# One half of an output projection with the activations standing and the weight streaming in four column tiles, in a decode kernel on one Trainium2 core

## Chip, core and metric

The kernel runs on one core of one Trainium2 chip. The metric is the device time of one execution in microseconds (us); several executions of the kernel are timed and their median is the time. The profile used beside it is one further execution, recorded by the hardware profiler.

## What is computed

One decode step for 8 sequences (B = 8, one token each, D = 512). Only the last W = 2048 positions of the two caches are read. Cut to what matters:

```python
x = A_x                                               # 8 x 1 x 512
h = x + attention(layernorm(x), k_cache, v_cache, wq) @ wo
# attention: 32 query heads of 128, 8 key/value heads, softmax over 2048 positions
# wo: 4096 x 512, so the projection sums over 32 heads x 128
u = layernorm(h)
h2 = h + u + gelu(layernorm(u) @ w3) @ w4             # w3: 512 x 1792, w4: 1792 x 512
```

The token-shift branch with w1 and w2 is identically zero for one token and isn't computed.

## The kernel before, in words

**Units.** The attention is cut into 16 units n = 0..15: unit n is sequence b = n // 2 and half t = n % 2 of the eight key/value heads (16 query heads). Each unit loads 2 MB of keys (`knat`) and 2 MB of values (`vnat`). All loads of caches and weights are issued by SyncE (SP) from one function, line 204, into one DMA queue, so that they land nearly in the order of issue: the last of them are the values of unit 15, the second half of wo, two pieces of w3 and four pieces of w4.

**Main loop (lines 549 to 593).** Keys are turned on TensorE by fp32 transposes (line 313), copied out by ScalarE and VectorE (lines 300 and 301) and multiplied with the queries in four column tiles of 32 (line 328: 32 columns standing, 512 moving). Softmax runs once for a sequence. The values are multiplied three units late (line 425; for the last three units line 415 with the values standing). `fold` and `turn_o` bring a unit's result into `o2`: on VectorE the scaling (line 448) and a spread (line 455), on TensorE a turn in four column tiles (line 464), on VectorE a mask (line 471) and a sum (line 477). `o2[:, t, j, b]` then holds, on 128 partitions, element block j (of 16) of half t of sequence b.

**Output projection.** `pe_wo(t)` (lines 508 to 516) multiplies half t of wo (2048 rows, seen as 16 blocks j of 128 rows). For every j and each of four column blocks nb it loads a 128 x 128 block of wo as the standing operand and streams the 8 columns of `o2[:, t, j, :]` past it: 64 pairs of a weight load and a matmul for a half, all accumulated in `hT_ps`, which is 128 partitions x 32 (four blocks nb x 8 sequences), so that the result h lies transposed. Before it, `pe_wo_x` (line 504) adds x into the same place.

**Order at the end (lines 608 to 615).** Each engine works its list in the order in which the program appends to it. For TensorE the end of the list is: line 415 for the last unit, `pe_wo(0)`, the turn of the last unit (line 464), `pe_wo(1)`, then layernorm sums (lines 640 and 662), w3 (line 657), one fp32 matmul that puts the residual into `z_ps` (line 682) and w4 in four column tiles (line 691). `pe_wo(0)` waits for the sum of unit 14 (line 477) and for the first half of wo, loaded since unit 7; `pe_wo(1)` waits for the sum of unit 15 and for the second half of wo (`sem_wl`). On ScalarE the last entry before the tail is a one-element square root (line 615), which loads the table that lines 663 and 664 need. Lines 700 and 702 copy the result out, line 705 stores it.

Two more things that the change uses: `oE`, a 128 x 512 fp32 tile which in the main loop takes the copied-out value products (line 434) for `fold` (line 443: fp32 matmuls with 128 columns of `oE` standing and 16 columns of `selo` moving); and `selo`, 128 x 32, with a one where the partition number modulo 32 equals the column.

Of the kernel before, what the change touches and what calls it, by code (L numbers as in the profile page):

```python
# [6 lines left out]
dt = mybir.dt  # L7
ACT = mybir.ActivationFunctionType
ALU = mybir.AluOpType
AX = mybir.AxisListType  # L10

B = 8
# [11 lines left out]
KC = D // 128  # L24
# [4 lines left out]
NU = 2  # L29
# [11 lines left out]
KR = 16  # L41
# [6 lines left out]
NST = 3  # L48
# [33 lines left out]
def bass_sequential_preLN__sliding_block_cached__mixer_s_mlp__decode_kernel(  # L82
# [19 lines left out]
    NUN = NB * NU  # L102
# [4 lines left out]
    with es:  # L107
        sb = lambda shape, dtype, name: es.enter_context(nc.sbuf_tensor(name, shape, dtype))
# [7 lines left out]
        wo_v = wbig[:, :].rearrange("p (t j n) -> p t j n", t=NU, j=KR)  # L116
# [44 lines left out]
        oM = sb([128, KR, QR], dt.bfloat16, "oM")  # L161
        oE = sb([128, 512], dt.float32, "oE")
        selo = sb([128, MO], dt.float32, "selo")
        o2 = sb([128, NU, KR, B], dt.bfloat16, "o2")

        NH = KC * B
        tail = Pz[:, 0, :].bitcast(dt.float32)
# [2 lines left out]
        def tl(n, bf=False):  # L170
# [14 lines left out]
        kbank = [kT_ps[i // 2][:, (i % 2) * 1024:(i % 2 + 1) * 1024].bitcast(dt.float32) for i in range(4)]  # L185
# [10 lines left out]
        sem_wl = S("sem_wl")  # L196
        sem_w3 = [S(f"sem_w3{i}") for i in range(2)]
        sem_x, sem_wq, sem_wo, sem_w4a, sem_w4b, sem_w4c, sem_out = (
            S(n) for n in ("sem_x", "sem_wq", "sem_wo", "sem_w4a", "sem_w4b", "sem_w4c", "sem_out"))
        PE, AC, DV, PO, SP = (Engine(S(n)) for n in ("s_pe", "s_act", "s_dve", "s_pool", "s_sp"))  # L200

        def dma(eng, dst, src, sem, *waits):
            def f(e):
# [7 lines left out]
        e_iota = PO.op(lambda e: e.iota(iota_f, [[1, 128]], base=0, channel_multiplier=-1,  # L211
                                        allow_small_or_imprecise_dtypes=True))
        e_qz = PO.op(lambda e: e.memset(qz[:], 0.0))
        PO.op(lambda e: e.memset(ones_f[:], 1.0))
        PO.op(lambda e: e.memset(ones_m[:], -1.0 / D))
        PO.op(lambda e: e.memset(eps2[:], EPS * EPS))
# [5 lines left out]
        e = DV.op(lambda e: e.bn_stats(st6[:, :], x_sb[:, :]), X)  # L222
        e = DV.op(lambda e: e.bn_aggr(mv[:, :], st6[:, :]), e)
        e = AC.op(lambda e: e.activation(rstd[:, :], mv[:, 1:2], ACT.Sqrt, bias=eps1[0:B, :], scale=1.0), e, e_eps)
        e = DV.op(lambda e: e.reciprocal(rstd[:, :], rstd[:, :]), e)
# [6 lines left out]
        e_selo = DV.op(lambda e: e.tensor_reduce(selo[:, :], ident_f[:, :].rearrange("p (a x) -> p x a", a=TO),  # L232
                                                 AX.X, ALU.add))
# [25 lines left out]
        e = PE.op(pe_xT, e_xln, e_idb)  # L259
# [12 lines left out]
        e = DV.op(lambda e: e.tensor_scalar(q_d, S_ps[0][:, 0:H * B], inv_sqrt_dh, None, ALU.mult), e_q)  # L272
# [17 lines left out]
        e_T, e_Tlo, e_Thi, e_lo, e_hi, e_QK, e_PV = {}, [], [], [], [], {}, {}  # L290
        e_ev, e_Pz = {}, {}
        e_max, e_mT, e_neg, e_negps, e_negc, e_exp, e_PT, e_pS, e_lsel, e_Lb, e_rL, e_scale, e_sc = ({} for _ in range(13))
# [112 lines left out]
        e_ev_o, e_fold, e_turn = {}, {}, {}  # L405
# [52 lines left out]
        def turn_o(n):  # L458
            b, t = divmod(n, NU)
            dst = sm[:, 0:QR * KR]  # L460

            def f(e):
                for r in range(R):
                    ins = e.matmul(dst[32 * r:32 * (r + 1), :], mE[:, :],
                                   oK[:, n % 2, QR * r:QR * (r + 1), :].rearrange("p h j -> p (h j)"),
                                   start=True, stop=True, tile_position=(0, 32 * r), skip_group_check=True)
                return ins
            e_turn[n] = PE.op(f, e_mE, e_sc[n], sm_read[0])
            m_ap = mH[:, :]
            m_bc = bass.AP(tensor=m_ap.tensor, offset=m_ap.offset, ap=[m_ap.ap[0], [0, KR], [1, QR]])  # L470
            e = DV.op(lambda e: e.tensor_tensor(oM[:, :, :], dst.rearrange("p (h j) -> p j h", h=QR), m_bc, ALU.mult),
                      e_turn[n], e_mH, e_scale.get(n - 1))
            sm_read[0] = e

            def g(e):
                with nc.allow_low_precision(reason="one term and zeros"):
                    return e.tensor_reduce(o2[:, t, :, b], oM[:, :, :], AX.X, ALU.add)
            e_scale[n] = DV.op(g, e)

        def load_k(n):  # L480
            b, t = divmod(n, NU)
# [9 lines left out]
        def load_wo(t, sem):  # L491
            dma(SP, wo_v[:, t, :, :].rearrange("p j n -> p (j n)"),
                A_wo[128 * KR * t:128 * KR * (t + 1), :].rearrange("(p j) n -> p (j n)", j=KR), sem, e_q)

        def hcol(nb):
            at = 256 * (nb // 2) + nb % 2
            return slice(at, at + 255, 2)

        hT_ps = S_ps[0]
        e_wo = []  # L500

        def pe_wo_x(e):
            for nb in range(KC):
                ins = e.matmul(hT_ps[:, nb * B:(nb + 1) * B], x_sb[:, hcol(nb)],
                               ident_b[0:B, 0:B], start=(nb == 0), stop=False, skip_group_check=True)
            return ins

        def pe_wo(t, *waits):
            def f(e):
                for j in range(KR):  # L510
                    for nb in range(KC):
                        ins = e.matmul(hT_ps[:, nb * B:(nb + 1) * B], wo_v[:, t, j, hcol(nb)],  # L512
                                       o2[:, t, j, :], start=False, stop=(t == NU - 1 and j == KR - 1),
                                       skip_group_check=True)
                return ins
            e_wo.append(PE.op(f, *waits))

        def emit_PV(i):
            n, w = divmod(i, U)
# [19 lines left out]
        def turn_os(to):  # L539
            while turned[0] < to:  # L540
                turn_o(turned[0])
                turned[0] += 1
# [6 lines left out]
        for n in range(NUN):  # L549
# [8 lines left out]
            i = U * n  # L558
            b, t = divmod(n, NU)
# [49 lines left out]
        PE.op(pe_wo_x, e_exp[NB - 2], X)  # L609
        emit_PVs(NBLK)  # L610
        load_wo(1, sem_wl)
        pe_wo(0, e_scale[NUN - NU], (sem_wo, 16))
        turn_os(NUN)
        pe_wo(1, e_scale[NUN - 1], (sem_wl, 16))
        e_gl = AC.op(lambda e: e.activation(scratch[:, 1:2], scratch[:, 0:1], ACT.Sqrt), e_warm)

        for a in range(2):
# [16 lines left out]
        def bc(a, k=KC):  # L634
            return bass.AP(tensor=a.tensor, offset=a.offset, ap=[a.ap[0], [0, k], [1, B]])
# [6 lines left out]
        e = DV.op(lambda e: e.tensor_tensor(v3(hc[:, :]), v3(hs[:, :]), bc(st1), ALU.add))  # L642
        e = DV.op(lambda e: e.tensor_tensor(hsq[:, :], hc[:, :], hc[:, :], ALU.mult), e)
# [18 lines left out]
        e = PE.op(lambda e: e.matmul(st2, ones_v[:, :], vsum[:, :], start=True, stop=True), e_vs, e_sc[NUN - 1])  # L662
# [4 lines left out]
        e = DV.op(lambda e: e.tensor_tensor(v3(xb[:, :]), v3(hc[:, :]), bc(rr[:, B:2 * B]), ALU.mult), e_r1)  # L667
# [5 lines left out]
        for n in range(2):  # L673
            cs = slice(n * FH * B, (n + 1) * FH * B)
            gs = slice(n * FH * 32, (n + 1) * FH * 32)
            e = DV.op(lambda e, n=n, cs=cs: e.tensor_tensor(v3(g_x[:, cs]), v3(y_ps[n][:, 0:FH * B]),
                                                            bc(rr[:, 0:B], FH), ALU.mult), e_y[n], e_rr)
# [64 lines left out]
```

## Time and profile before

| What | us |
|---|---|
| median of 3 runs | 195.41 (195.14 to 195.58) |
| the profiled execution | 195.09 |
| its span, first to last instruction | 193.8 |
| outside its span | 1.29 |
| TensorE busy in the span | 145.7 (75%) |
| VectorE busy | 107.6 (56%) |
| ScalarE busy | 89.9 (46%) |
| HBM read | 79.18 MB, 409 GB/s over the span |

How to read the profile's lines. Times are from the span's start. A line of the timeline gives start, duration, engine, line of the kernel, operation, the tile written and the tiles read, shapes and a count; PE is a matmul on TensorE, PEld its weight load, DVE is VectorE, ACT is ScalarE; in brackets stands how long the engine was idle before and what ended that. "128*32" is the used part of the array (rows * columns). An fp32 matmul that isn't a transpose shows as two records for PE and two for PEld. "issue" is idle time for which the profile shows no cause. PEclk is the granted TensorE clock as a share of full speed. In the view by windows, after the length of the window, each engine has its busy time and in brackets its number of instructions; the last three columns are PEclk, DMA share and GB/s.

### The profile page before, as it was taken

What the parts mean: (1) busy time and instruction counts of PE and PEld (TensorE: products, weight loads), DVE (VectorE), ACT (ScalarE), POOL (GpSimd) and SP (SyncE); (2) the same over time, 40 slices, a digit from 0 to 9 for tenths busy, and PEclk for the clock granted to TensorE, in tenths of its full rate; (3) what the DMA queues carried; (4) which work ended last, traced back from release to release, by engine and by line L of the source; (5) the groups of instructions that cost most, each with busy time, mean ns of one, the idle gap of its engine ahead of it and who ended that gap; (6) DMA issues with size and microseconds to landing.
All of it is one profiled execution on the core that took longest, in us unless ns stands there. A gap on an engine that the chain in (4) does not pass through costs nothing.

```text
span 193.8 us, 4487 instructions
## 1 busy us (share of the span) xinstructions
PE 145.7 (75%) x1972; PEld 114.9 (59%) x1972; DVE 107.6 (56%) x281; ACT 89.9 (46%) x115; POOL 7.8 (4%) x29
## 2 busy tenths in 40 slices
PE   0028985978899799918887897886597897768675
PEld 0037862866568477608575866564585574667674
DVE  5502445476596687722966485657355965843232
ACT  6000566747547485524464636482354664250022
POOL 5001001000100100010001000100000000000000
PEclk9999999699999999975999799999879999655555
DMA  6999999999999999999999999999999999999981
GB/s 225 433 430 430 430 433 430 423 426 421 423 430 423 423 433 424 426 426 430 430 430 423 430 426 426 426 421 433 433 409 430 426 426 430 426 426 424 406 353 54
DMA packets 5954, 79.46 MB, mean 410 GB/s; under 512 B 672, under 2 KB 688, under 8 KB 1456
## 3 DMA queue, kind: packets, MB, share of 16 engines
q1 hardware_dynamic: 5920, 79.18, 96.6%
q8 instruction: 15, 0.25, 0.5%
q14 instruction: 3, 0.02, 0.0%
q10 hardware_dynamic: 16, 0.01, 0.0%
HBM read 79.18 MB, written 0.01 MB: 409 GB/s over the span
## 4 chain that ended last, share of the span: by engine, by line
DMA 51%; PE 33%; DVE 13%; issue 2%; ACT 0%; SPq 0%
DMA knat<-in_A_k_cache_dram 44%; PE kT_ps L313 17%; DMA vnat<-in_A_v_cache_dram 7%; DVE kT_sb L301 6%; PE S_ps L328 5%; DVE Pz L374 3%; PE kT_ps L385 3%; PE S_ps L512 2%; DVE mcol L338 1%; PE oT_ps L415 1%; PE kT_ps L657 1%; PE S_ps L691 1%; PE sm L443 1%; DVE Mrow L344 1%; PE sm L342 1%
## 5 line engine op out<-in xcount | busy, mean ns | idle before, releaser
L300 ACT ACTIVATE kT_sb<-kT_ps 128x1024 bf16<-128x1024 bf16 x64 | 62.8, 1023 | 42.5 <-PE kT_ps L313 42.4
L313 PE MATMUL kT_ps<-perm_k,knat 128*128 128x128 f32 x512 | 71.8, 299 | 10.0 <-DMA knat<-in_A_k_cache_dram 9.7
L313 PEld LDWEIGHTS kT_ps<-perm_k,knat 128*128 128x128 f32 x512 | 63.7, 154 | 17.4 <-DMA knat<-in_A_k_cache_dram 11.3
L301 DVE TENSOR_SCALAR kT_sb<-kT_ps 128x512 int32<-128x512 int32 x64 | 43.5, 688 | 38.4 <-PE kT_ps L313 38.3
L328 PE MATMUL S_ps<-kT_sb,qz 128*32 128x512 bf16 x256 | 19.8, 383 | 6.3 <-DVE kT_sb L301 4.2
L374 DVE TENSOR_TENSOR Pz<-P_sb,mJ 128x256 bf16<-128x256 bf16 x64 | 23.9, 417 | 0.0
L434 ACT ACTIVATE oE<-oT_ps 128x256 f32<-128x256 f32 x13 | 5.0, 384 | 27.8 <-PE oT_ps L425 27.8
L425 PE MATMUL oT_ps<-vnat,pS 128*32 128x256 bf16 x416 | 17.5, 275 | 0.3 <-DMA vnat<-in_A_v_cache_dram 0.3
L300 ACT ACTIVATE pS<-kT_ps 128x1024 bf16<-128x1024 bf16 x8 | 8.2, 1024 | 10.5 <-PE kT_ps L385 10.5
L328 PEld LDWEIGHTS S_ps<-kT_sb,qz 128*32 128x32 bf16 x256 | 4.6, 94 | 11.3 <-ACT kT_sb L300 10.2
L425 PEld LDWEIGHTS oT_ps<-vnat,pS 128*32 128x32 bf16 x416 | 9.1, 96 | 3.4 <-DMA vnat<-in_A_v_cache_dram 0.4
L301 DVE TENSOR_SCALAR pS<-kT_ps 128x512 int32<-128x512 int32 x8 | 5.5, 691 | 7.7 <-PE kT_ps L385 7.7
L385 PE MATMUL kT_ps<-perm_p,Pz 128*128 128x128 f32 x64 | 9.6, 298 | 0.0
L285 POOL COPY qz<-q_sb 64x64 bf16<-64x64 bf16 x16 | 4.7, 291 | 117.4 <-PE S_ps L328 101.6
L385 PEld LDWEIGHTS kT_ps<-perm_p,Pz 128*128 128x128 f32 x64 | 7.6, 151 | 3.0 <-issue 3.0
L267 PE MATMUL S_ps<-xlnT,wbig 128*128 128x8 bf16 x128 | 3.6, 168 | 7.7 <-DMA wbig<-in_A_wq_dram 7.7
L443 PEld LDWEIGHTS sm<-selo,oE 128*128 128x128 f32 x52 | 7.9, 217 | 0.4 <-ACT oE L434 0.4
L267 PEld LDWEIGHTS S_ps<-xlnT,wbig 128*128 128x128 bf16 x128 | 3.5, 104 | 7.7 <-issue 7.7
L415 PE MATMUL oT_ps<-pS,vnat 128*128 128x16 bf16 x192 | 6.3, 175 | 2.4 <-DMA vnat<-in_A_v_cache_dram 1.5
L338 DVE TENSOR_REDUCE mcol<-S_ps 128x1 f32<-128x512 f32 x8 | 5.5, 692 | 4.5 <-PE S_ps L328 4.5
L443 PE MATMUL sm<-selo,oE 128*128 128x16 f32 x52 | 7.7, 263 | 0.3 <-DVE negcol L356 0.3
L415 PEld LDWEIGHTS oT_ps<-pS,vnat 128*128 128x128 bf16 x192 | 5.9, 105 | 3.1 <-DMA vnat<-in_A_v_cache_dram 1.9
(93 smaller groups left out, 94.5 us busy)
## 6 DMA issues: line engine op xcount, KB each, us to landing
knat<-in_A_k_cache_dram SPq DMA_DIRECT2D x16, 2048.0 KB, 30.0
vnat<-in_A_v_cache_dram SPq DMA_DIRECT2D x16, 2048.0 KB, 34.2
wbig<-in_A_wq_dram SPq DMA_DIRECT2D x1, 4096.0 KB, 12.2
wbig<-in_A_wo_dram SPq DMA_DIRECT2D x2, 2048.0 KB, 24.9
knat<-in_B_w_dram SPq DMA_DIRECT2D x2, 896.0 KB, 20.3
knat<-in_B_w_dram SPq DMA_DIRECT2D x3, 512.0 KB, 22.7
knat<-in_B_w_dram SPq DMA_DIRECT2D x1, 256.0 KB, 23.6
x_sb<-in_A_x_dram ACTq DMA_DIRECT2D x1, 8.0 KB
```

The lines of the kernel that those rows point to most:

```text
L267: ins = e.matmul(S_ps[0][:, h * B:(h + 1) * B], wq_v[:, kc, h * DH:(h + 1) * DH], xlnT[:, kc * B:(kc + 1) * B], start=(kc == 0), stop=(kc ...
L300: e_lo.append(AC.op(lambda e: e.activation(dst[:, 0:1024], ps[:, 0:1024], ACT.Copy), e_Tlo[k], *free))
L301: e_hi.append(DV.op(lambda e: e.tensor_single_scalar(dst[:, 1024:2048].bitcast(dt.int32), ps[:, 1024:2048].bitcast(dt.int32), 0, ALU.bitwi ...
L313: ins = e.matmul(ps[:, c * 128:(c + 1) * 128], src[:, c * 128:(c + 1) * 128], perm_k[:, :], is_transpose=True)
L328: ins = e.matmul(S_ps[b % 2][32 * j:32 * (j + 1), :].rearrange("p (c r) -> p c r", c=16), qz[:, b % 2, J * t + j, k, lo:lo + 32], kT[:, j, k],
L338: e_max[b] = DV.op(lambda e: e.tensor_reduce(mcol[:, :], S_ps[b % 2][:, :], AX.X, ALU.max), e_QK[4 * b + 3], e_mT.get(b - 1))
L374: e_Pz[b, part] = DV.op(lambda e, o=o, p_bc=p_bc, m_bc=m_bc: e.tensor_tensor(Pz[:, 0, J * o:J * (o + 64)].rearrange("p (x j k) -> p x j k" ...
L385: ins = e.matmul(ps[:, c * 128:(c + 1) * 128], src[:, c * 128:(c + 1) * 128], perm_p[:, :], is_transpose=True)
L415: ins = e.matmul(oT_ps[:, 0:16], vnat[:, n % NV, (16 * w + c) * DH:(16 * w + c + 1) * DH], pS[:, b % 2, o:o + 31:2], start=(w == 0 and c = ...
L425: ins = e.matmul(oT_ps[MO * q:MO * (q + 1), NO * (n % 2):NO * (n % 2 + 1)], pS[:, b % 2, o:o + 2 * MO - 1:2], vnat[:, n % NV, (16 * w + 2 ...
L434: e_ev_o[n] = AC.op(lambda e: e.activation(oE[:, NO * (n % 2):NO * (n % 2 + 1)], oT_ps[:, NO * (n % 2):NO * (n % 2 + 1)], ACT.Copy), e_PV[ ...
L443: ins = e.matmul(sm[:, 32:48], oE[:, o:o + 128], selo[:, 16 * s:16 * s + 16], start=(s == 0), stop=(s == 2 * VP - 1))
```

## The change

The first half of wo is computed the other way round. `o2` becomes two tiles. The one for half 0 has 32 columns for each block j, of which 8 are used; a new memset on GpSimd at the start sets it to zero, and the sum of line 477 waits for that. `pe_wo_0` has, for every j, the 32 columns of o as the standing operand and the whole 128 x 512 block of wo moving: 16 matmuls, dealt out to the four column tiles, accumulated on 32 partitions each of one bank (`kbank[1]`, used before for turned keys). ScalarE copies this 128 x 512 result to `oE`, ahead of its one-element square root. The second half stays as it was, but is cut in two; between its 32nd and 33rd pair stand four fp32 matmuls (`pe_fold_0`), which have 128 columns of `oE` standing and 8 columns of `selo` moving: each adds the four tiles together, turns them and accumulates into `hT_ps`.

On TensorE, 64 pairs of weight load and matmul become 16 pairs ahead of the last turn, and 8 pairs (four fp32 matmuls of two records) within the second half. The order of all else on TensorE, VectorE, ScalarE and SyncE stays.

```diff
-        o2 = sb([128, NU, KR, B], dt.bfloat16, "o2")
+        o2 = [sb([128, KR, n], dt.bfloat16, f"o2{i}") for i, n in enumerate((32, B))]
...
+        e_oz = PO.op(lambda e: e.memset(o2[0][:], 0.0))
...
-                    return e.tensor_reduce(o2[:, t, :, b], oM[:, :, :], AX.X, ALU.add)
-            e_scale[n] = DV.op(g, e)
+                    return e.tensor_reduce(o2[t][:, :, b], oM[:, :, :], AX.X, ALU.add)
+            e_scale[n] = DV.op(g, e, e_oz)
...
-        def pe_wo(t, *waits):
-            def f(e):
-                for j in range(KR):
-                    for nb in range(KC):
-                        ins = e.matmul(hT_ps[:, nb * B:(nb + 1) * B], wo_v[:, t, j, hcol(nb)],
-                                       o2[:, t, j, :], start=False, stop=(t == NU - 1 and j == KR - 1),
-                                       skip_group_check=True)
-                return ins
-            e_wo.append(PE.op(f, *waits))
+        h0_ps = kbank[1]
+
+        def pe_wo_0(e):
+            for j in range(KR):
+                q = j % 4
+                ins = e.matmul(h0_ps[32 * q:32 * (q + 1), :], o2[0][:, j, :], wo_v[:, 0, j, :],
+                               start=(j < 4), stop=(j >= KR - 4), tile_position=(0, 32 * q), skip_group_check=True)
+            return ins
+
+        def pe_fold_0(e):
+            for nb in range(KC):
+                ins = e.matmul(hT_ps[:, nb * B:(nb + 1) * B], oE[:, hcol(nb)], selo[:, 0:B],
+                               start=False, stop=False, skip_group_check=True)
+            return ins
+
+        def pe_wo_1(e, lo, hi):
+            for j in range(lo, hi):
+                for nb in range(KC):
+                    ins = e.matmul(hT_ps[:, nb * B:(nb + 1) * B], wo_v[:, 1, j, hcol(nb)],
+                                   o2[1][:, j, :], start=False, stop=(j == KR - 1), skip_group_check=True)
+            return ins
...
-        pe_wo(0, e_scale[NUN - NU], (sem_wo, 16))
+        e = PE.op(pe_wo_0, e_scale[NUN - NU], (sem_wo, 16), e_lo[-1], e_hi[-1], e_lo[-2], e_hi[-2])
+        f = e_fold[NUN - NST - 1]
+        e_h0 = AC.op(lambda e: e.activation(oE[:, :], h0_ps, ACT.Copy), e, f)
         turn_os(NUN)
-        pe_wo(1, e_scale[NUN - 1], (sem_wl, 16))
+        PE.op(lambda e: pe_wo_1(e, 0, KR // 2), e_scale[NUN - 1], (sem_wl, 16))
+        PE.op(pe_fold_0, e_h0, e_selo)
+        e_wo = [PE.op(lambda e: pe_wo_1(e, KR // 2, KR))]
```

More of the change, by code (lines that the diff above doesn't have):

```diff
@@ L499, in bass_sequential_preLN__sliding_block_cached__mixer_s_mlp__decode_kernel @@
         hT_ps = S_ps[0]
-        e_wo = []
         def pe_wo_x(e):
```

## The prediction

> **What bounds the kernel now.** I read the page first: DMA is at 9 tenths or more in nearly every slice but the last two, so the loads bound the whole and only the end, after the last loads, can move. So I took the chain of work that ended last, in order of time, from the last values on, then the timeline of the same stretch, then the landings.
>
> ```profile
> 177.46 0.05 issue
> 177.50 0.59 PE oT_ps L415 x16
> ...
> 180.04 1.01 issue
> 181.06 1.47 PE S_ps L512 x49
> 182.53 0.21 PE sm L464 x3
> ...
> 183.31 1.89 PE S_ps L512 x64
> ...
> 189.93 1.72 PE S_ps L691 x44
> ```
>
> The chain runs on TensorE, with short VectorE steps between. The first half of wo takes 179.50 to 182.46: 15 pairs, a gap of 1.01 us, 49 pairs. The last turn stands behind it, and the second half behind the turn. The timeline has the rows that this rests on:
>
> ```profile
> 178.58 0.23 DVE L477 TENSOR_REDUCE o<-oM 128x16 bf16<-128x64 bf16 x1
> 179.50 0.54 PE L512 MATMUL S_ps<-o,wbig 128*128 128x8 bf16 x15
> 179.89 0.42 DVE L455 TENSOR_TENSOR oK<-o,mK 128x256 bf16<-128x256 f32 x1
> 181.06 1.47 PE L512 MATMUL S_ps<-o,wbig 128*128 128x8 bf16 x49 [1.01 <-issue]
> 182.46 0.24 PE L464 MATMUL sm<-oK,mE 128*32 128x64 bf16 x4
> 183.31 1.87 PE L512 MATMUL S_ps<-o,wbig 128*128 128x8 bf16 x64 [0.60 <-DVE o L477]
> 191.21 0.14 PEld L691 LDWEIGHTS S_ps<-knat,Pz 128*32 128x32 bf16 x8 [0.15 <-DMA knat<-in_B_w_dram]
> ```
>
> Two landings fence this stretch in. The second half of wo is issued at 164.57 and, by the view of that tile (17.8 us to landing), is there at about 182.4. The last piece of w4 is there at about 191.2: the last row shows line 691 waiting for it. So the end is bound twice, by TensorE's chain and, within a tenth, by the last load: **a shorter TensorE chain gains at most about 0.1 us, a longer one costs nearly its full length.**
>
> The rows with the prices, from the timeline of short windows: two fp32 folds, one piece of w4, one score product.
>
> ```profile
> 168.16 1.01 PE L443 MATMUL sm<-selo,oE 128*128 128x16 f32 x4
> 189.86 1.47 PE L691 MATMUL S_ps<-knat,Pz 128*32 128x128 bf16 x48
> 92.76 0.62 PE L328 MATMUL S_ps<-kT_sb,qz 128*32 128x512 bf16 x8
> ```
>
> A pace is the duration of such a row, less one instruction's own, over the steps between. The clock is granted at 0.50 from 166.6 to the end, and at 1.00 at 92.76.
>
> **Part by part.**
>
> *Removed:* 64 pairs of line 512. The 64 in one piece take 1.87 us, one lasts 0.168, so 1.70/63 = 0.027 us a pair, 1.71 us in all, and the 1.01 us gap within them.
>
> *Added ahead of the turn:* 16 matmuls in four column tiles. Line 691 has the same form with 128 moving columns: 12 rounds of four, (1.47 - 0.31)/11 = 0.106 us a round at clock 0.50. For 512 columns that is four times as much, 0.42 us a round. Line 328, 512 columns at full clock, agrees: two rounds, 0.62 - 0.39 = 0.23 us, half of it at twice the clock. Four rounds are 1.70 us: as much as the 64 pairs. What is saved is thus the gap alone. It stands after 15 pairs of line 512, after the same count of instructions the first 15 of the 16 new pairs have been issued. So either the 16th waits until 181.06 and ends about 181.5, or there is no gap and the 16 end at 179.50 + 1.70 = 181.2. The turn, 182.46 now, then starts 0.95 to 1.25 us earlier, at 181.5 or 181.2; its oK (179.89 + 0.42) is long there. Line 464 to the second half takes 183.31 - 182.46 = 0.85 us, so o is ready by 182.05 to 182.35.
>
> *The second half's new wait.* It also needs its wo, at about 182.4. After a landing TensorE starts within 0.04 to 0.05 us (177.46 to 177.50 in the chain). So it starts at about **182.47, with or without the gap**: 0.84 us earlier than 183.31. Queued behind it on TensorE are the folds and all that follows.
>
> *The four fp32 folds.* Nothing hides them: they stand in TensorE's list, between two parts of a chain with no idle time. Line 443 has the same form at the same clock, 128 fp32 columns standing and few moving: (1.01 - 0.37)/3 = 0.213 us a record. Eight records: **+1.70 us**. Line 443's columns lie side by side and those of the fold at a step of two, which no fp32 row shows, so I bound it. From below, 0.027 us a record as on line 512: 0.21 us. From above, each weight load in the open: line 443's loads last 0.333 us at this clock, 2.66 us. I take 1.70: line 443 is the nearest in type, size and clock, and line 512's bf16 loads do step by two at 0.027.
>
> *ScalarE's copy.* 512 fp32 columns; line 359 takes 0.69 us for 512, line 434 0.38 for 256. Behind the first half it runs 181.7 to 182.4, and the fold needs it at 182.47 + 32 x 0.027 = 183.32: 0.9 us to spare, hidden by the first part of the second half. Without that cover it would cost what it is late by. Queued behind it is the square root of line 615 with its table load (1.28 + 0.20 us, now at 171.61): it ends about 183.9, and line 663 wants it after 187.5.
>
> *At nothing:* the memset (line 213 writes 1792 columns in 1.59 us, so some 0.45 us for 512; GpSimd waits 15.3 us there afterwards) and the new waits of line 477 and of the first half, all met many us before. SyncE's list and so every load is as before.
>
> **The sum.** TensorE's chain from the second half on: -0.84 + 1.70 = +0.86 us. The last piece of w4 is then no longer waited for: 12 rounds of line 691 from 189.86 end at 191.13, the next began about 191.21, so 0.08 us comes off. **+0.78 us.** On the profiled execution's own time, 195.09 (193.8 of span and 1.29 around it), that is 195.87. It lies 0.32 under the median of the runs, so I set the difference on the median: 195.41 + 0.78 = **196.2 us**.
>
> If a run of before has no gap, its TensorE is earlier but its end isn't (the last w4), and after is pinned by the second half of wo: the difference stays within 0.1 of this.
>
> **The rivals.**
>
> *The clock rises (not slower).* The new half streams more, so the throttle might let go, and the folds halve to about 0.11 us a record (line 443 at 164.80, at full clock: four records in 0.59 us, one lasting 0.26). That takes 0.8 us off the folds, and as much again off lines 640, 662, 682 and 691; the end meets the last w4, and the time is 195.3 to 195.4. [...] The clock's own history speaks against it:
>
> ```profile
> 33.43:36.85 3.42, 2.95 (x14) 2.93 (x15) 1.23 (x4) 1.80 (x3) 0.00 (x0) 0.50 1.01 426
> 36.85:40.26 3.41, 3.00 (x29) 2.17 (x27) 2.84 (x8) 2.75 (x3) 0.00 (x0) 1.00 1.00 428
> 187.03:190.45 3.42, 3.42 (x84) 3.20 (x88) 1.18 (x6) 2.21 (x5) 0.00 (x0) 0.50 0.56 222
> 190.45:193.80 3.35, 1.17 (x44) 0.75 (x32) 0.59 (x2) 0.61 (x2) 0.00 (x0) 0.50 0.02 7
> ```
>
> Fourteen transposes at 0.21 us, some 2.8 of 3.4 us of streaming, raised it; 84 short matmuls that kept PE busy throughout did not. The new half streams 1.3 us after 180.2, and no placing of a 3.4 us window holds more than its 1.7. I give 5%. [...]
>
> *The folds cost little (not slower).* At 0.21 us the chain would be 0.63 shorter, cut to 0.1 by the last w4: 195.3 to 195.4. Against: both rows of line 443 in fp32, at either clock. 5%.
>
> *The folds cost more,* by the step of two or by exposed loads: up to 2.66, so 197.2. For: line 657's loads with a step of four take 0.033 a pair instead of 0.027. 9%.
>
> *The copy is late,* by a table load of 1.28 us ahead of it: 182.4 + 1.28 is 0.36 after 183.32: 196.55. Against: line 434's copies show none after the exponential. 3%.
>
> *The tiles don't run side by side* with 512 columns at half clock, so that the change doesn't do what it says: 16 x 0.42 = 6.8 us, the second half from 187.2: about 200.9. Against: lines 691 and 328. 3%.
>
> **How the numbers follow.** The forecast, 195.9 to 196.5, has 75%. With the dearer fold, up to 197.1, it is 84%; I let the range begin at 195.7 for the scatter of the runs (195.14 to 195.58), and leave out the two cheap cases and the serial one. About 0.2%, 0.4 us, is what a measurement of this kernel can tell from no change. Faster by more needs an earlier last load, for which nothing speaks: 4%, and within 0.2% the clock, the cheap folds and scatter: 12%. Slower: 84%.
>
> **What would show it.** The first half as 16 matmuls in about 1.7 us from 179.5; the second half starting with the landing of its wo near 182.5; eight fp32 records at 0.21 us behind the 32nd pair; the sums of line 637 about 0.86 later; no wait left on line 691; PEclk 0.50. Wrong would be: PEclk 1.00 after 183.6, fold records well off 0.21, or a wait for ScalarE's copy ahead of them.

## The result and the profile after

| What | before | after |
|---|---|---|
| median of 11 runs, us | 195.41 (194.98 to 196.05) | 196.12 (195.83 to 197.06) |
| ratio, 95% interval | | 1.0044 (1.0026 to 1.0061) |
| profiled execution, us | 195.09 | 195.91 |
| its span, us | 193.8 | 194.6 |
| TensorE busy, us | 145.7 | 141.9 |
| TensorE weight loads and matmuls in the trace | 2 x 1972 | 2 x 1932 |

TensorE has 40 pairs less, and the kernel is slower: by 0.7 us by the two medians, by 0.9 us (0.5 to 1.2) by the ratio. The 3.8 us of busy time that TensorE has less are not the change's. They come from the main loop, 5.3 us less busy, where the transposes of line 313 (314 after) took 66.6 us instead of 71.8, in an execution with a mean granted clock of 0.912 instead of 0.886. From 179.45 us to the end TensorE was busy for 10.98 us, and for 9.43 before.

The timeline of the end of the changed kernel (the profile calls the bank of the first half kT_ps, `hT_ps` and `z_ps` S_ps, and w3 and w4, which lie where keys lay, knat):

```profile
179.50 2.07 PE L512 MATMUL kT_ps<-wbig,o 128*32 128x512 bf16 x16
180.96 0.10 PEld L512 LDWEIGHTS kT_ps<-wbig,o 128*32 128x32 bf16 x1 [0.47 <-issue]
181.61 0.60 ACT L625 ACTIVATE oE<-kT_ps 128x512 f32<-128x512 f32 x1 [10.10 <-PE sm L465]
181.93 0.23 DVE L478 TENSOR_REDUCE o<-oM 128x16 bf16<-128x64 bf16 x1
182.53 0.99 PE L525 MATMUL S_ps<-o,wbig 128*128 128x8 bf16 x32 [0.90 <-DMA wbig<-in_A_wo_dram]
183.38 1.85 PE L518 MATMUL S_ps<-selo,oE 128*128 128x8 f32 x8
185.09 0.99 PE L525 MATMUL S_ps<-o,wbig 128*128 128x8 bf16 x32
190.77 1.68 PE L706 MATMUL S_ps<-knat,Pz 128*32 128x128 bf16 x56
```

The first half of wo now takes 16 matmuls (line 512) in the place of 64; o of the last unit is ready at 182.16 (181.93 + 0.23). The second half (line 525) doesn't start then: what ends its idle time is the landing of wo. The eight fp32 records (line 518) stand bare between its two parts. The last matmuls (line 706) run in one piece of 1.68 us with no wait for w4. The chain that ended last says the same from the other side. It goes back to a DMA, the second half of wo, and from there on TensorE and VectorE take turns, up to ScalarE's copies out. It begins:

```profile
164.16 18.23 DMA wbig<-in_A_wo_dram
182.39 0.14 issue
182.53 0.99 PE S_ps L525 x32
183.52 1.71 PE S_ps L518 x8
185.23 0.86 PE S_ps L525 x32
```

By windows, the clock stayed at half, with TensorE busier in the first of these two than it was there before (2.52 us against 1.96):

```profile
180.20:183.62 3.42, 2.52 (x50) 1.41 (x42) 0.50 (x3) 1.98 (x3) 0.00 (x0) 0.50 1.00 417
183.62:187.03 3.41, 3.06 (x42) 2.88 (x42) 0.32 (x3) 0.10 (x1) 0.00 (x0) 0.50 1.00 401
```

### The profile page after: what moved, and what is told of

It reads as the page before. It is cut to its first block, busy times and chain, and to the rows that moved or that the text cites. A ratio compares the mean times of both kernels' runs of the same rounds, so it can differ in the third digit from the quotient of the medians.

```text
span 194.6 us, 4410 instructions
## 1 busy us (share of the span) xinstructions
PE 141.9 (73%) x1932; PEld 109.9 (56%) x1932; DVE 107.8 (55%) x281; ACT 89.9 (46%) x116; POOL 8.2 (4%) x30
## 4 chain that ended last, share of the span: by engine, by line
DMA 56%; PE 27%; DVE 14%; issue 1%; ACT 0%; SPq 0%
DMA knat<-in_A_k_cache_dram 46%; PE kT_ps L314 14%; DMA wbig<-in_A_wo_dram 9%; DVE kT_sb L302 6%; PE S_ps L329 4%; DVE Pz L375 3%; PE kT_ps L386 2%; DVE mcol L339 1%; PE S_ps L525 1%; PE kT_ps L672 1%; PE S_ps L518 1%; PE S_ps L706 1%; DVE Mrow L345 1%; PE sm L343 1%; DVE oK L456 1%
## 5 line engine op out<-in xcount | busy, mean ns | idle before, releaser
L314 PE MATMUL kT_ps<-perm_k,knat 128*128 128x128 f32 x512 | 66.6, 285 | 14.3 <-DMA knat<-in_A_k_cache_dram 14.0
L314 PEld LDWEIGHTS kT_ps<-perm_k,knat 128*128 128x128 f32 x512 | 58.8, 146 | 22.0 <-DMA knat<-in_A_k_cache_dram 16.1
L444 PEld LDWEIGHTS sm<-selo,oE 128*128 128x128 f32 x52 | 7.2, 202 | 0.4 <-ACT oE L435 0.4
```

The costliest lines, as they stand in the source:

```text
L314: ins = e.matmul(ps[:, c * 128:(c + 1) * 128], src[:, c * 128:(c + 1) * 128], perm_k[:, :], is_transpose=True)
L444: ins = e.matmul(sm[:, 32:48], oE[:, o:o + 128], selo[:, 16 * s:16 * s + 16], start=(s == 0), stop=(s == 2 * VP - 1))
```

## The experiments

Each kernel was timed in five rounds with before on the same chip; the ratio is to before, with its 95% interval. Before's median there was 195.30 us for the first three kernels of the table and for before without the first half, and 195.19 for all others.

| Kernel | us | ratio to before | interval |
|---|---|---|---|
| after without folds | 195.11 | 0.9984 | 0.9970 to 0.9998 |
| after with bf16 folds | 195.07 | 0.9984 | 0.9968 to 1.0001 |
| bf16 folds ahead of the second half | 195.13 | 0.9988 | 0.9973 to 1.0002 |
| fp32 folds ahead of the second half | 195.87 | 1.0031 | 1.0010 to 1.0051 |
| before without the first half of wo | 195.18 | 0.9986 | 0.9974 to 0.9998 |
| after without the last piece of w4 | 196.05 | 1.0034 | 1.0018 to 1.0050 |
| bf16 folds ahead, no last w4 | 194.90 | 0.9981 | 0.9964 to 0.9998 |
| the same, 36 pairs more at the start | 194.75 | 0.9979 | 0.9959 to 0.9999 |
| bf16 folds ahead, 36 pairs more at the start | 195.08 | 0.9994 | 0.9978 to 1.0009 |
| before, 16 pairs more at the start | 197.21 | 1.0099 | 1.0069 to 1.0129 |

### Are the folds the loss?

**Left out.**

```diff
-        PE.op(pe_fold_0, e_h0, e_selo)
```

> The changed kernel without its four fp32 folds, so the first half of wo is left out of the output. Forecast's theory (the folds' eight records of 0.213 us lie bare on TensorE's chain, and the last piece of w4 is a floor under the end): the chain is 1.70 us shorter, the last w4 (landing at 191.1) is waited for again, and the time falls only back to before's: 195.2 to 195.5, ratio to before 0.999 to 1.000. Rival A (the folds are partly hidden, the loss is made elsewhere in the new half): it stays at 195.8 or more, ratio 1.002 or more. Rival B (no floor): the whole 1.70 us comes off, 194.4, ratio 0.995.

Measured: 195.11, ratio 0.9984. With the folds gone the time is back at before's, or a little under it. 1.71 us came off TensorE's list and 1.0 us off the time (196.12 to 195.11, measured apart; by the ratios 0.0060 x 195.3 = 1.2). So the loss lies in the folds, rival A is out, and rival B with its 194.4 too. In the execution that was profiled, the last values ran 1.2 us later than in the changed kernel (178.60 instead of 177.42), and the second half started at 183.28, behind o and not behind its landing at 182.71. The end came no later for that: it hung on the last w4, as the next section shows.

**In bf16, in the same place.**

```diff
-                ins = e.matmul(hT_ps[:, nb * B:(nb + 1) * B], oE[:, hcol(nb)], selo[:, 0:B],
+                ins = e.matmul(hT_ps[:, nb * B:(nb + 1) * B], oE_b[:, hcol(nb)], selo_b[:, :],
...
-        e_h0 = AC.op(lambda e: e.activation(oE[:, :], h0_ps, ACT.Copy), e, f)
+        e_h0 = AC.op(lambda e: e.activation(oE_b[:, :], h0_ps, ACT.Copy), e)
```

> The changed kernel with one type changed: the copy of the first half's result and the ones it is folded with are bf16 instead of fp32, so the folds are four pairs of bf16 in the same place. Forecast's theory: a pair costs 0.027 us as on the second half's pairs, 0.11 us instead of 1.70 in all; time as without folds, 195.2 to 195.5, ratio 0.999 to 1.000, the pairs seen at 0.027 us. Rival A (what costs is the stop in the second half and the wait for ScalarE's copy, not the fp32 type): a gap stays before or behind the four pairs and the time is 195.8 or more.

Measured: 195.07, ratio 0.9984. The timeline of that kernel (line 521 is the fold):

```profile
182.42 0.99 PE L528 MATMUL S_ps<-o,wbig 128*128 128x8 bf16 x32 [0.72 <-DMA wbig<-in_A_wo_dram]
183.28 0.25 PE L521 MATMUL S_ps<-selo_b,oE_b 128*128 128x8 bf16 x4
183.38 0.99 PE L528 MATMUL S_ps<-o,wbig 128*128 128x8 bf16 x32
188.59 0.31 PE L674 MATMUL kT_ps<-Pz,knat 128*128 128x8 bf16 x6 [0.26 <-issue]
```

From the fold's first matmul to the pair behind it are 0.10 us, with no gap on either side, where the fp32 folds took 1.71. It is the type that costs, not the stop. (The copy in bf16 rounds the sums of the first half to bf16.) The last row is a new gap in the middle of w3; it comes up again below.

**In bf16 and ahead of the second half.**

```diff
-        PE.op(lambda e: pe_wo_1(e, 0, KR // 2), e_scale[NUN - 1], (sem_wl, 16))
         PE.op(pe_fold_0, e_h0, e_selb)
-        e_wo = [PE.op(lambda e: pe_wo_1(e, KR // 2, KR))]
+        e_wo = [PE.op(lambda e: pe_wo_1(e, 0, KR), e_scale[NUN - 1], (sem_wl, 16))]
```

> As the bf16 fold, but the four pairs stand ahead of the second half, where TensorE idled from 181.4 to 182.5 in the changed kernel. The copy is there at about 182.2, so the folds end at about 182.4 and cost nothing. Forecast's theory: second half at 182.5 as in the changed kernel, its sums 0.1 us before those of the bf16 fold in the middle, the end still at the last w4: 195.2 to 195.45, the same as with the bf16 fold in the middle within 0.1, ratio 0.999 to 1.000. Rival B (no floor): 0.1 less than in the middle and 0.9 less than before.

Measured: 195.13, ratio 0.9988, the same as in the middle. In its timeline the four pairs run at 182.09 and the second half starts at 182.40, just behind the landing of its wo at 182.26: the folds are free there, and nothing is gained by it.

**In fp32 and ahead of the second half,** with the copy in two parts:

```diff
+        e_h0 = AC.op(lambda e: e.activation(oE[:, 0:256], h0_ps[:, 0:256], ACT.Copy), e, f)
+        e_h1 = AC.op(lambda e: e.activation(oE[:, 256:512], h0_ps[:, 256:512], ACT.Copy))
...
+        PE.op(lambda e: pe_fold_0(e, 0), e_h0, e_selo)
+        PE.op(lambda e: pe_fold_0(e, 2), e_h1)
+        e_wo = [PE.op(lambda e: pe_wo_1(e, 0, KR), e_scale[NUN - 1], (sem_wl, 16))]
```

> The changed kernel with its fp32 folds moved ahead of the second half, where TensorE waits for the second half of wo, and the copy cut into two of 256 columns, so that the first two folds can begin at about 182.05. Forecast's theory: eight records of 0.213 us end at 183.75 and the 64 pairs of the second half follow in one piece; the sums come at 183.75 + 1.71 + 0.2 = 185.65 instead of 186.12, so 0.3 to 0.5 us off the changed kernel: 195.5 to 195.9, ratio to before 1.001 to 1.003. Rival A (the stop inside the second half is what costs): back to before's time or below, ratio 1.000 or less.

Measured: 195.87, ratio 1.0031: between before and after, as the theory had it, at the upper edge of what was expected, and the interval holds after's 1.0044 too, so this run alone doesn't tell the two apart. The folds ran from 182.34 and not from 182.05, because in this execution the matmuls of the last values began at 177.89, behind line 456, and not at 177.42 behind their landing:

```profile
182.34 1.88 PE L518 MATMUL S_ps<-selo,oE 128*128 128x8 f32 x8 [0.44 <-ACT oE L625]
184.07 1.85 PE L525 MATMUL S_ps<-o,wbig 128*128 128x8 bf16 x64
```

### Is the last landing the floor?

**Before without the first half of wo.**

```diff
-        pe_wo(0, e_scale[NUN - NU], (sem_wo, 16))
```

> The kernel before with the first half of wo left out (64 pairs and its part of the output). TensorE can turn the last unit at 180.4 instead of 182.46. Forecast's theory (the second half waits for its wo at 182.4, the end for the last w4 at 191.2): TensorE's chain is 0.84 us earlier from the second half on, but the time falls by 0.1 us at most, 195.2 to 195.45, ratio 0.999 to 1.000, with a longer wait for w4 on line 691's last matmuls. Rival B (the chain on TensorE alone sets the end): 0.8 us less, 194.6, ratio 0.996.

Measured: 195.18, ratio 0.9986. Taking all 64 pairs and the gap out of before's end gains 0.1 to 0.3 us, not 0.8. Its timeline shows where the rest went:

```profile
180.48 0.25 PE L464 MATMUL sm<-oK,mE 128*32 128x64 bf16 x4 [0.72 <-DVE oK L455]
182.55 1.90 PE L512 MATMUL S_ps<-o,wbig 128*128 128x8 bf16 x64 [1.82 <-DMA wbig<-in_A_wo_dram]
189.43 2.17 PE L690 MATMUL S_ps<-knat,Pz 128*32 128x128 bf16 x56 [0.23 <-DMA knat<-in_B_w_dram]
190.55 0.35 PEld L690 LDWEIGHTS S_ps<-knat,Pz 128*32 128x32 bf16 x16 [0.35 <-DMA knat<-in_B_w_dram]
191.19 0.14 PEld L690 LDWEIGHTS S_ps<-knat,Pz 128*32 128x32 bf16 x8 [0.28 <-DMA knat<-in_B_w_dram]
```

The turn is 2.0 us earlier than in before, and the second half only 0.76: it waits 1.82 us for its wo. Line 690, the product with w4, starts only when the first two pieces of w4 have landed (189.29) and takes 2.17 us instead of after's 1.68, for within it stand the waits for the two later pieces, in the last two rows. So a shorter first half has two landings to run into. The end hangs on the second: the copies out begin 0.50 us after the last piece of w4 has landed, here (191.15 and 191.65) and in before (191.17 and 191.67), and 0.50 to 0.51 us after it in all kernels with all of w4 whose folds are left out or in bf16. In the changed kernel they begin 1.39 us after it (191.12 and 192.51).

**After without the last load,** and its counterpart.

```diff
-        dma(SP, w4_sb[:, FA:FC, :].rearrange("p c n -> p (c n)"),
-            B_w4[FA * 128:F, :].rearrange("(p c) n -> p (c n)", c=FC - FA), sem_w4c)
```

> The changed kernel without the load of the last piece of w4 (its two blocks are multiplied with what lies there from the keys). Forecast's theory (TensorE's chain with the bare folds sets the end, 0.8 us after the last landing): no change within 0.1 us, 196.0 to 196.2, ratio to before 1.003 to 1.005. If the last landing sets this kernel's end: 0.6 us off, 195.5.

> The kernel with the bf16 folds ahead of the second half, without the load of the last piece of w4 (256 KB; its two blocks are multiplied with what lies there from the keys). If the last landing is the floor under this kernel, the end moves to the landing before it, 0.6 us earlier: 0.5 to 0.7 us off, 194.5, ratio to before 0.996. If TensorE's chain sets its end: no change, 195.1.

Measured: after without it 196.05, ratio 1.0034, as after; its end hangs on TensorE. The bf16 kernel without it 194.90: 0.2 us less than with it, where 0.5 to 0.7 were expected. The last landing did move, from 191.35 to 190.38, but 0.34 us of this lie between the two executions: the last piece itself takes 0.63 (190.72 to 191.35). And 24 matmuls of the product wait for the new last landing instead of 8; 16 more are four rounds of 0.106, 0.42 us, which leaves 0.21. This kernel also had a gap of its own, on line 671 within w3:

```profile
188.58 0.31 PE L671 MATMUL kT_ps<-Pz,knat 128*128 128x8 bf16 x6 [0.34 <-issue]
189.46 1.80 PE L705 MATMUL S_ps<-knat,Pz 128*32 128x128 bf16 x56
```

**The same with 36 more pairs at the start,** to move that gap away (why this should do it is the next section):

```diff
-        e = PE.op(pe_xT, e_xln, e_idb)
+        PE.op(pe_xT, e_xln, e_idb)
+        for _ in range(8):
+            PE.op(pe_xT)
+        e = PE.op(pe_xT)
```

> The kernel with bf16 folds ahead and without the last piece of w4, with 36 more pairs of weight load and matmul on TensorE at the very start (the turn of the normalised x done ten times), where it idles before wq lands. Theory: that kernel lost its 0.6 us to the wait for the next 256 instructions, 0.34 us bare in the middle of w3; 72 instructions more move the two late counts to the last values (178.9) and to the start of w3 (186.6), where the instructions should be there in time: no gap of over 0.2 us after 178, time 194.4 to 194.7, 0.2 to 0.5 less than without the shift. Rival (the gap does not matter, another floor): 194.9 as without.

> The kernel with bf16 folds ahead of the second half, all of w4 loaded, with the same 36 more pairs at the start. Theory (the last landing of w4 is the floor, not the wait for instructions): within 0.15 us of it without the shift, 195.0 to 195.2, ratio to before 0.998 to 0.999. Rival (TensorE's chain with its gap sets the end): 0.3 us less, 194.8, ratio 0.997.

Measured: without the last w4 194.75, with it 195.08. The gap is gone in both (w3 runs in one piece of 1.95 us), and each is within 0.15 us of its unshifted twin, which these intervals don't tell apart; for the one without the last w4 a gain of 0.2 to 0.5 was expected and is not shown. The traces say why: with and without the 36 pairs, its copies out begin 0.93 us after the landing that the last 24 matmuls wait for (190.39 and 191.32, 190.38 and 191.31), so the gap of 0.34 us had cost nothing. Of the kernels that compute the whole output, those with bf16 folds came out at 0.9984, 0.9988 and 0.9994, and all three intervals hold 1: none is a gain on before that can be told. The timeline of the one with all of w4 and the 36 pairs ends on the landings again:

```profile
189.10 2.19 PE L710 MATMUL S_ps<-knat,Pz 128*32 128x128 bf16 x56 [0.23 <-DMA knat<-in_B_w_dram]
```

### What is the gap after 15 pairs?

**Before with 16 more pairs at the start.**

```diff
-        e = PE.op(pe_xT, e_xln, e_idb)
+        PE.op(pe_xT, e_xln, e_idb)
+        PE.op(pe_xT)
+        PE.op(pe_xT)
+        PE.op(pe_xT)
+        e = PE.op(pe_xT)
```

> The kernel before with 16 more pairs of weight load and matmul on TensorE at the very start (the turn of the normalised x done five times), long before anything waits for them: 32 instructions more ahead of the end. Theory of the gap: it is the wait for the next 256 instructions, which falls on fixed counts of TensorE's list. Then the 1.0 us gap after 15 pairs of the first half goes, and one of 0.5 to 1.2 us stands 16 pairs earlier, at the start of the first half; the next count then falls some 5 pairs before the end of the second half, where the following instructions would be 0.5 to 2 us late: time 195.4 to 196.6. Rival: the gap belongs to the first half itself (its operands or its place): it stays after 15 pairs and the time is before's.

Measured: 197.21, ratio 1.0099: 16 pairs of 0.027 us, done while TensorE had nothing else to do, cost 2.0 us. The timeline of the end (line 419 is the last values, 516 wo):

```profile
180.89 0.17 PE L419 MATMUL oT_ps<-pS,vnat 128*128 128x16 bf16 x1 [0.96 <-issue]
181.02 1.85 PE L516 MATMUL S_ps<-o,wbig 128*128 128x8 bf16 x64
183.64 1.71 PE L516 MATMUL S_ps<-o,wbig 128*128 128x8 bf16 x58 [0.60 <-DVE o L481]
187.17 0.31 PE L516 MATMUL S_ps<-o,wbig 128*128 128x8 bf16 x6 [1.82 <-issue]
```

The gap moved 16 pairs ahead, to one matmul before the end of the last values, and the first half runs whole. A second gap of 1.82 us opened six pairs before the end of the second half. Both were expected there; the time is over the expected 196.6, because 65 pairs instead of 49 now stand between the first gap and the turn (second half at 183.64 instead of 183.31) and the second gap came out near the top of its bounds. Together they put the copies out at 193.90 instead of 191.67, 2.2 us later. Counted in the traces, weight loads, matmuls and recorded waits of TensorE's list together, the gaps stand behind number 3520 in before, 3520 in after (0.2 us, ahead of the 16th matmul), 3776 with the bf16 folds, and 3520 and 3776 here: always on a multiple of 256 less 64.

The page's third part has 15 packets of 0.25 MB in all on the instruction queue, 16 KB each. In before's trace one runs from 178.57 to 179.66, and the matmul behind the gap starts at 181.06; here the two run 178.41 to 179.52 and 184.82 to 185.92, with matmuls again at 180.89 and 187.17. No view names this wait, but the counts, the packets and the shift agree: TensorE waits for its next 256 instructions. Ahead of the gaps of 1.01, 0.96 and 1.82 us the packet starts 3.1 to 5.0 us after the count 256 earlier was passed, takes 1.1, and the instructions run 1.2 to 1.5 us later: 5.6 to 7.6 us in all, while 128 pairs at 0.027 us are used up in 3.5. In before's trace all 15 packets start 1.2 to 4.5 us behind such a count (192, 448 and so on up to 3776), and at one count alone, 3520, does the view of that trace's matmul waits list idle time without a cause, 1.0 us. In this stretch, then, the wait lies bare: 0.96 and 1.82 us of it here, while the DMA share was 0.99 to 1.03.

## Why the prediction was right, point by point

Forecast 196.2, measured 196.12; on the profiled execution 195.87 and 195.91. The difference of 0.78 came out as 0.71 by the medians and 0.86 by the ratio.

- *The 16 matmuls cost as much as the 64 pairs.* Right: rounds of four start at 179.50, 179.91, 180.33 and 180.76, 0.42 us apart. The gap kept its place in the list, ahead of the 16th matmul, but was 0.2 us long, since the first 15 took the time that the instructions needed. The turn came 1.27 us earlier, just over the 0.95 to 1.25 worked out: the 1.01 us are the idle time after the 15th pair's end, and the starts on its two sides lie 1.18 apart.
- *The second half starts at 182.47, with its landing.* It started at 182.53, 0.14 us behind the landing at 182.39 and not 0.05. Before without the first half, and after without the last w4, start it 0.13 us behind the landing too. The prediction's 0.05 came from another landing, that of the last values.
- *Eight records of 0.213 us, bare.* Right: (1.85 - 0.36)/7 = 0.213. The step of two in the standing columns, which no row had shown, costs nothing.
- *The copy is hidden.* It ran 181.61 to 182.21, with 1.1 us to spare; the table load behind it ended at 183.5 and nobody waited for it.
- *The sums 0.86 later, 0.08 less at the end.* Measured 186.12 against 185.21, which is 0.91, and the copies out at 192.51 against 191.67, which is 0.84. The 0.07 between them is the wait for the last w4, gone as forecast.
- *The rivals.* The clock stayed at 0.50, with 2.52 us of PE busy in the window before 183.62. In before's trace it changes at 33.43, 36.85, 84.63, 91.46, 108.53, 111.94, 139.25, 142.66 and 166.55 us, always a whole number of steps of 3.41 us apart, and 180.20 and 183.62 lie on the same steps. What raises it at a step no run shows: PE was busy for 2.95 to 3.42 us in the step ahead of each of the four rises, and for 3.42 us in the one ahead of 190.45, where it stayed at 0.50. The cheap fold exists, but as bf16, and its time is then near the rival's: 195.07 measured, 195.3 to 195.4 worked out. One reading under the clock's rival was off by one: the window from 33.43 holds 13 transposes, 2.75 us, and its 14th instruction is another; against the 1.7 of the new half the argument stands with 2.75, as the author's estimate.
- *A shorter chain gains at most 0.1 us.* Nearly: the runs with a shorter chain came out at 0.9984 to 0.9994, 0.1 to 0.3 us under before, with intervals that reach from 0.2 us over it to 0.6 under. In the traces nothing is gained, for before's copies out begin 0.50 us after the last landing already; where the 0.1 to 0.3 of the times comes from stays open.

Of 1.27 us won on the turn (181.19 instead of 182.46), 0.78 reached the second half (182.53 instead of 183.31), and 1.71 was then given out on the folds: the change took its gain in a place where a landing cut it off, and paid in one where nothing hides it.

## What to carry to other kernels

Before an edit on a chain near the end, write down the landings that the chain meets. They say how much of a gain can arrive, and a cost arrives whole but for what waits behind it can take up (0.07 us here). When a few wide matmuls replace many narrow ones, price what brings the result back into the old layout first: here four fp32 matmuls cost as much as the 64 pairs they helped to save, and in bf16 a sixteenth of that. Where a busy engine idles for about a microsecond without a cause in the profile, count its instructions. Here such places stood at fixed counts, 256 apart, and 16 or 36 pairs more at the start moved them.

## What the runs showed of the hardware

16 harmless pairs at the start of TensorE's list cost 2.0 us at its end, through the place where the next 256 instructions fall due; 36 pairs, in the kernel with bf16 folds ahead, cost nothing that can be told (195.08 against 195.13). A change that alters the count of instructions can thus move the time by a per cent for a reason that isn't in it.

At a granted clock of 0.50 an fp32 record with 128 standing columns took 0.213 us, with the columns side by side (line 443) or at a step of two (line 518) alike, against 0.027 us for a bf16 pair.
